# Linear attention and a top-2 mixture of experts: key transposes by single heads, gate products by quarters turned on VectorE

## The chip, the core and the metric

The kernel runs on one core of a Trainium2 chip. The metric is the device time of one execution in microseconds (us). The time of the kernel before is the median of three runs; the profile shows one execution of it.

## What is computed

First, decayed linear attention over 4 batches, 8 heads, 768 positions and 64 dimensions, in blocks with a carried state; then a mixture of 8 experts over the 3072 tokens of 512 features, of which each token uses two.

```python
intra = np.einsum('bhic,bhjc->bhij', qb, kb) * Dmask[None]
intra = np.einsum('bhij,bhjd->bhid', intra, vb)
inter = np.einsum('bhid,bhde->bhie', qb * lam_pow[None], kv_state)
out[:, :, sl] = intra + inter
kv_state = lam_block[None, :, None, None] * kv_state + np.einsum('bhsd,bhse->bhde', kb_dec, vb)

x = np.ascontiguousarray(attn_out.transpose(0, 2, 1, 3)).reshape(B * S, H * D)
logits = x @ w_gate
noise_scale = np.log1p(np.exp(x @ w_noise))
noisy_logits = logits + noise_scale * noise
# top 2 of 8 per token, softmax over the two as weights
h = np.maximum(x[mask] @ w1[e], 0.0)
out[mask] += top2_w[mask, k, None] * (h @ w2[e])
```

## The kernel before

**Stages.** The attention runs in 12 steps of 256 tokens (two chunks of 128; NST = 12), three steps to a batch. The loop over t (L981 to L1043) finishes step t and prepares step u = t + 1. Behind it the experts follow, one after the other, each as two matrix products over gathered token rows (gemm1, gemm2).

**One turn of the loop, in program order, which is the order on every engine.** The schedule is manual: instructions stand on each engine's queue as the code issues them.

1. trans_k(u) (L319): the keys of step u lie with two neighbouring positions and 64 dimensions of a head in one row. TensorE transposes 128 columns at a time into banks pS. Three sets of four transposes are made: one that takes the second position of one head and the first of the next, and two of which only one half is used. ScalarE (VectorE for u = 0) evacuates the three banks into kT, one in full, two by halves. In kT the index y mixes head parity and position, so scores (L372) reads kT at x ^ s.
2. kv(u) (L412): products of decayed keys and values; the first chunk goes to a bank pS, the second to bank pR. A step that ends a batch (u = 2, 5, 8, 11) has the first chunk alone. state(u) on VectorE (L431) adds them to the carried states.
3. trans_q(u) (L334): eight transposes; ScalarE copies them, VectorE scales them (qTs).
4. advance(FILLS): VectorE works off a budget of queued jobs (the gate of eight chunks, its routing, the lists of tokens), if there are any. Jobs are queued at t = 4, at t = 8 and after the loop, one group of tokens each (GB = 0, 8, 16, 24).
5. intra(t), inter(t, 0): the outputs of step t in banks pO and pKV; evac_o on ScalarE writes xo.
6. store_x(t - 1): eight transposes of xo, evacuated by ScalarE (xc) and stored by SyncE's DMA queue (SP) to x_tok in memory.
7. products(t - 1) (L434): gate and noise weights (32 columns) times xo. Four matmuls with 256 moving columns, one for each block of 128 features, each to its own 32 partitions of bank pR. ScalarE copies pR to xp (L440).
8. scores(u) (L372) into four banks pS; VectorE multiplies each by the decay mask (at, L375). Then inter(u, 1).
9. logits(t - 1) (L456): for each chunk one matmul with xp as weights and a selector of 16 columns (sel) adds the four blocks and turns tokens to partitions, into bank pL. The gate's first job copies the logits from there (L476).
10. advance(FILL): again a budget of jobs on VectorE.

There are four banks pS in rotation and one each of pR, pO, pKV and pL. A product into a bank waits until its last reader is done.

**Tokens and partitions.** In the gate, partition p of chunk c is token 128 c + p; noise (nz, L1043), the token numbers for the lists (rowf, tokb, L243 to L248, loads, decode) and the store of the gate weights (store_w, L548) all use this. store_w writes 8 weights of 4 bytes to each row of x_tok with one DMA per group; the expert gathers rows of x_tok afterwards.

**After the loop.** The first matmuls of expert 0 (mm1), products(11), store_w(1), store_x(11), the remaining jobs, logits(11), the lists (enlist, bank pR), and then the evacuations evac1 on ScalarE (L901) and VectorE (L905) into ht, which lies where xc lay before.

Of the kernel before, what the change touches and what calls it, by code (L numbers as in the profile page):

```python
# [21 lines left out]
FT = mybir.dt.float32  # L22
# [37 lines left out]
HOT = 2 * (128 + NTL + NV * NTL)  # L60
NST = NCH // 2
NW = NC // 2
MAXOV = 40
ARENA = 1304
MAXT = 24
OPUS = 0.21
FILL, SPLIT, FILLS = 2.0, 1.2, 3.4
# [25 lines left out]
def sub(ap, offset, dims):  # L93
    return bass.AP(tensor=ap.tensor, offset=ap.offset + offset, ap=dims)
# [31 lines left out]
def kernel(  # L126
# [90 lines left out]
    def mask(s, h, c):  # L217
# [25 lines left out]
    nc.gpsimd.iota(rowf, pattern=[[0, 1]], base=-TS, channel_multiplier=1, allow_small_or_imprecise_dtypes=True)  # L243
    tokb = consts.tile([128, NCH, NV], BF, name="tokb")
    nc.gpsimd.iota(tokb[:, :, 0], pattern=[[1, NCH]], base=-(BIG // TS), channel_multiplier=0,
                   allow_small_or_imprecise_dtypes=True)
    nc.gpsimd.iota(tokb[:, :, 1], pattern=[[0, NCH]], base=-TS, channel_multiplier=1,
                   allow_small_or_imprecise_dtypes=True)  # L248
    destf = consts.tile([128, 2, NCH], FT, name="destf")
    recs = consts.tile([128, NTL], I32, name="recs")  # L250
    sel = consts.tile([128, 2 * E], FT, name="sel")

    def make_sel():

        v = nc.vector
        v.tensor_scalar(sel, jp[:, 0:2 * E], 0.0, None, op0=OP.is_equal)
        for q in range(1, DB):
            v.tensor_scalar(sq4, jp[:, 0:2 * E], float(-32 * q), None, op0=OP.is_equal)
            v.tensor_add(sel, sel, sq4)

    sq4 = ac.tile([128, 2 * E], FT, name="sq4")

    class Arena:

        def __init__(self, n):
# [13 lines left out]
            return v  # L279

    arena = Arena(ARENA)
    for s, w in ((0, w_gate), (1, w_noise)):
# [33 lines left out]
    def half(i):  # L316
        return slice(i * 64, (i + 1) * 64)

    def trans_k(u, banks=()):  # L319

        banks = iter(banks)
        kT[u] = aw.tile([128, HP, 2, C], FT, name="kT", bufs=1)
        flat = KT[u].rearrange("p h x d -> p (h x d)")
        for at, y, r in ((D, 1, slice(0, 128)), (0, 0, half(0)), (2 * D, 0, half(1))):
            nm = next(banks, None)
            p = psum.tile([128, HP, C], FT, name=nm) if nm else bank()
            for hp in range(HP):
                nc.tensor.transpose(p[:, hp, :], flat[:, hp * 4 * D + at:hp * 4 * D + at + 2 * D], identf)  # L328
            if u:
                nc.scalar.activation(kT[u][r, :, y, :], p[r], AF.Copy)  # L330
            else:
                nc.vector.tensor_copy(kT[u][r, :, y, :], p[r])

    def trans_q(u, banks=()):  # L334

# [26 lines left out]
    def scores(u):  # L362
        AT[u] = []
        for r in range(2):
            at = aw.tile([128, 2, 2, 2, C], FT, name="at")
            AT[u].append(at)
            ps = [bank().rearrange("p (h x) i -> p h x i", x=2) for _ in range(2)]
            for h in range(2):
                for x in range(2):
                    for s in range(2):  # L370
                        for a in range(2):
                            nc.tensor.matmul(ps[s][half(a), h, x, :], kT[u][half(s), 2 * r + h, x ^ s, half(a)],  # L372
                                             qT[u][half(s), 2 * r + h, a * C:(a + 1) * C], start=True, stop=True)
            for s in range(2):
                nc.vector.tensor_mul(at[:, s], ps[s], mask(s, slice(2 * r, 2 * r + 2), slice(0, C)))  # L375
# [80 lines left out]
    def logits(u):  # L456
        nonlocal pl
        for a in range(2):
            g = 2 * u + a
            b = max(i for i in range(NG) if GB[i] <= g)  # L460
            if not g:
                pl = psum.tile([128, 512], FT, name="pL")
            if g == GB[b]:
                PL[b] = pl[:, NV * NTL:][:, :GM * 2 * E].rearrange("p (c e) -> p c e", e=2 * E)
                PC[b] = pl[:, NV * NTL + GM * 2 * E:]
            nc.tensor.matmul(PL[b][:, g - GB[b], :], XP[u][:, a, :], sel, start=True, stop=True)


    def gate(b):
# [4 lines left out]
        pl = PL[b]  # L474
        l2 = t([128, gs, 16], "l2")
        v.tensor_copy(l2, pl[:, :gs, :])  # L476
        yield
# [139 lines left out]
    def loads(b, c, n, buf):  # L617

        _, hi, mv = hot(buf, n)
        mv = mv.rearrange("p k (w j) -> p k w j", w=NV)  # L620
        nc.vector.tensor_scalar(mv[:, :, 1, :], hi, rowf, None, op0=MULT)
        for i in range(n):
            k = slice(2 * i, 2 * i + 2)
            nc.vector.tensor_scalar(mv[:, k, 0, :], hi[:, k, :], float(GB[b] + c + i - BIG // TS), None, op0=MULT)

    found = consts.tile([128, NV, NTL], FT, name="found")

# [15 lines left out]
    def decode(s, out, n):  # L643

        v = nc.vector
        idf = rp.tile([128, n], FT, name=f"idf{n > 1}")
        v.scalar_tensor_tensor(idf, s[:, 0], float(TS), s[:, 1], op0=MULT, op1=ADD)
        v.tensor_scalar(out, idf, float(BIG + TS), None, op0=ADD)

    def read_lists(a, b):  # L650
# [10 lines left out]
    kdecay(0)  # L661
    load(2, "kt")
    load(2, "vt")
    trans_k(1, ("pO", "pKV", "pL"))
    trans_q(1, ("pO", "pKV"))
    keep_warm(WARM[1])
    kv(0)
    kdecay(1)
# [13 lines left out]
        nc.vector.tensor_add(xo, xo, PO[0][0][half(g), g::2, :])  # L682
    kv(1)
    state(1)
    make_sel()
    inter(1, 1)

    def places(b):
# [292 lines left out]
    for t in range(NST):  # L981
# [16 lines left out]
        if not t:  # L998
            pass
        elif u < NST:  # L1000
            advance(FILLS)
        else:
            store_x(t - 1)
            products(t - 1)
            for j in range(PARTS0[0]):
                trans_rows(0, j)
            logits(t - 1)
            advance(FILLS)
        if t:
            intra(t)  # L1010
# [29 lines left out]
        if t >= NST - 2:  # L1040
            zero_out(3)
        if t == 2:
            nc.sync.dma_start(nz, sub(noise, 0, [[E, 128], [128 * E, NCH], [1, E]]))  # L1043
    assert got
    finish(1)
    head = [mm1(0, 0, PARTS0[0], 0)]
# [280 lines left out]
```

## Time and profile before

| | us |
|---|---|
| median of three runs | 718.95 |
| lowest and highest | 718.71, 720.71 |
| span of the profiled execution | 716.8 |
| TensorE busy | 698.8 |
| VectorE busy | 398.3 |
| GpSimd busy | 361.8 |
| ScalarE busy | 223.3 |

The span runs from the first to the last instruction of the profiled execution; no other time of its own is given for that execution, and the median lies 2.15 us above the span. The attention takes about the first 140 us, the experts the rest. The mean granted clock of TensorE is 0.994. Busy shares are averages over these stages, so a stage is read by itself.

### The profile page before, as it was taken

Reading aid. Unit: us, or ns where it says so; the run is one execution under the profiler, and the core shown is the slowest. Engines: PE = TensorE matmul, PEld = TensorE weight load, DVE = VectorE, ACT = ScalarE, POOL = GpSimd, SP = SyncE. Lnnn points to the kernel's source line nnn. Section 1 sums busy time; section 2 is a strip of 40 time slices with the busy share of each in tenths; the row PEclk is TensorE's granted clock in tenths of the full one; section 3 lists DMA queues with packets and bytes.
Section 4 is the critical chain, followed back from the end, with each engine's and each line's share of the span. In section 5 each row is a group of like instructions: output and inputs, shape, how many; then the busy total and the mean of one; then the engine's idle time right before and its main releaser. Section 6 shows DMA issues by size and latency. Waiting matters only on the chain.

```text
span 716.8 us, 15851 instructions
## 1 busy us (share of the span) xinstructions
PE 698.8 (97%) x6014; PEld 600.4 (84%) x6014; DVE 398.3 (56%) x1044; ACT 223.3 (31%) x382; POOL 361.8 (50%) x505
## 2 busy tenths in 40 slices
PE   7899999999999999999999999999999999999994
PEld 5888888889898898988888888888888898888883
DVE  4755899879355546743674367337624662565210
ACT  2255545542143312332233214222322242223100
POOL 4411342313453865687768567836773768321221
PEclk9999999999999999999999999999999999999998
DMA  9998986580645725273627352735452554330110
GB/s 203 263 230 245 251 232 203 188 305 25 180 131 168 207 56 179 82 185 87 183 93 176 85 186 84 176 88 161 116 154 79 170 143 122 104 116 30 51 51 32
DMA packets 94192, 104.32 MB, mean 146 GB/s; under 512 B 41234, under 2 KB 66844, under 8 KB 94112
## 3 DMA queue, kind: packets, MB, share of 16 engines
q1 hardware_dynamic: 79456, 65.73, 34.0%
q0 software_dynamic: 13552, 37.00, 17.0%
q10 hardware_dynamic: 1104, 0.53, 0.5%
q8 instruction: 49, 0.80, 0.5%
q14 instruction: 31, 0.25, 0.1%
HBM read 78.28 MB, written 26.12 MB: 146 GB/s over the span
## 4 chain that ended last, share of the span: by engine, by line
PE 89%; issue 4%; DMA 2%; POOL 1%; DVE 1%; ACTq 0%; SPq 0%; ACT 0%; POOLq 0%
PE pS L895 37%; PE pKV L933 16%; PE pO L933 16%; PE pO L384 3%; PE pS L372 3%; PE pS L328 2%; PE pS L450 2%; PE pO L938 2%; PE pS L419 2%; PE pS L344 1%; PE pKV L384 1%; PE pKV L938 1%; DMA Mk<-powd 1%; PE pR L438 1%; PE pS L874 1%
## 5 line engine op out<-in xcount | busy, mean ns | idle before, releaser
L839 POOL DMA_INDIRECT xg<-x_tok,recq x147 | 161.0, 1095 | 45.6 <-issue 40.0
L895 PE MATMUL pS<-xth,w1h 128*128 128x512 f32 (+3 forms) x544 | 181.4, 333 | 0.9 <-DVE ht L905 0.9
L895 PE MATMUL pS<-xth,w1l 128*128 128x512 f32 (+3 forms) x544 | 180.5, 332 | 0.0
L895 PE MATMUL pS<-xtl,w1h 128*128 128x512 f32 (+3 forms) x544 | 180.5, 332 | 0.0
L905 DVE SCALAR_TENSOR_TENSOR ht<-pS,ht 128x256 fp32r<-128x256 f32 (+3 forms) x176 | 75.8, 454 | 123.1 <-ACT ht L901 120.7
L933 PE MATMUL pKV<-w2h,ht 128*128 128x512 f32 x384 | 122.6, 390 | 0.0
L933 PE MATMUL pO<-w2h,ht 128*128 128x512 f32 x384 | 122.4, 390 | 0.0
L952 POOL DMA_INDIRECT out_dram<-ot,rec x46 | 60.7, 1319 | 121.0 <-DVE ot L945 110.8
L901 ACT ACTIVATE ht<-pS 128x512 fp32r<-128x512 f32 (+3 forms) x136 | 65.2, 483 | 173.2 <-PE pS L895 167.7
L895 PEld LDWEIGHTS pS<-xth,w1h 128*128 128x128 f32 x544 | 102.7, 189 | 10.4 <-DVE ht L905 1.1
L895 PEld LDWEIGHTS pS<-xth,w1l 128*128 128x128 f32 x544 | 102.7, 189 | 8.8
L895 PEld LDWEIGHTS pS<-xtl,w1h 128*128 128x128 f32 x544 | 102.7, 189 | 8.8
L933 PEld LDWEIGHTS pO<-w2h,ht 128*128 128x128 f32 x384 | 72.1, 188 | 14.9
L933 PEld LDWEIGHTS pKV<-w2h,ht 128*128 128x128 f32 x384 | 72.1, 188 | 14.9
L866 ACT ACTIVATE xth<-turned 128x512 fp32r<-128x512 f32 (+1 forms) x39 | 23.7, 607 | 167.5 <-DVE turned L864 167.5
L933 PE MATMUL pKV<-w2l,ht 128*128 128x512 f32 x192 | 74.9, 390 | 0.0
L933 PE MATMUL pO<-w2l,ht 128*128 128x512 f32 x192 | 74.8, 390 | 0.0
L360 POOL TENSOR_TENSOR kd<-kt,Mk 128x512 f32<-128x512 f32 x24 | 24.8, 1051 | 73.4 <-PE pR L419 51.6
L917 POOL DMA_INDIRECT pv<-out_dram,rec x46 | 47.0, 1021 | 14.2 <-issue 12.0
L375 DVE TENSOR_TENSOR at<-pS,Mk 128x512 f32<-128x512 f32 x48 | 29.9, 683 | 23.0 <-PE pS L372 18.5
L808 DVE TENSOR_TENSOR w2l<-wst,w2h 128x1024 fp32r<-128x1024 f32 (+1 forms) x33 | 39.2, 1191 | 6.1 <-ACT w2h L807 5.6
L933 PEld LDWEIGHTS pKV<-w2l,ht 128*128 128x128 f32 x192 | 36.1, 188 | 7.4
(241 smaller groups left out, 941.5 us busy)
## 6 DMA issues: line engine op xcount, KB each, us to landing
wst<-in_moe_w_dram SPq DMA_DIRECT2D x36, 512.0 KB, 4.2
wst<-in_moe_w_dram SPq DMA_DIRECT2D x96, 128.0 KB, 3.7
x_tok<-xc SPq DMA_DIRECT2D x24, 272.0 KB, 4.7
kt<-in_k_dram SPq DMA_DIRECT2D x12, 512.0 KB, 5.2
qt<-in_q_dram SPq DMA_DIRECT2D x24, 256.0 KB, 5.2
vt<-in_v_dram SPq DMA_DIRECT2D x12, 512.0 KB, 5.7
out_dram<-zero SPq DMA_DIRECT2D x24, 256.0 KB, 3.6
xg<-x_tok,recq POOLq DMA_INDIRECT x147, 2.8
```

The lines of the kernel that those rows point to most:

```text
L360: nc.gpsimd.tensor_mul(kd[:, :, s], kt[:, :, s], mask(s, slice(0, HP), slice(C - 1, C)).to_broadcast([128, HP, 2, D]))
L375: nc.vector.tensor_mul(at[:, s], ps[s], mask(s, slice(2 * r, 2 * r + 2), slice(0, C)))
L384: nc.tensor.matmul(PO[u][a][half(g), hp, :], lhs, rhs, start=n == 1, stop=n == (8 if not (u % NW or a) else 12 if u else 10))
L808: nc.vector.tensor_tensor(lo[:, r], st[:, r], hi[:, r].bitcast(FT), op=SUB)
L839: nc.gpsimd.indirect_dma_start(out=XG[t][:, g * QW:(g + 1) * QW], out_offset=None, in_=x_tok.rearrange("t (q w) -> (t q) w", w=QW), in_off ...
L866: nc.scalar.activation(hi, raw, AF.Copy)
L895: nc.tensor.matmul(p, W1[a][d][:, fs], xt(b, cs)[:, d], start=(d == 0 and i == 0), stop=(d == DB - 1 and i == 2))
L901: nc.scalar.activation(ht(e, 0, f, cs), p, AF.Relu)
L905: nc.vector.scalar_tensor_tensor(ht(e, 1, f, c), p[:, r], 0.0, ht(e, 0, f, c).bitcast(FT), op0=OP.max, op1=SUB)
L917: nc.gpsimd.indirect_dma_start(out=PV[t][:size(e, t), :], out_offset=None, in_=out, in_offset=bass.IndirectOffsetOnAxis(ap=REC[e, t], axis=0),
L933: nc.tensor.matmul(p, ht(e, a, f, cs), W2[b][f // 2][:, f % 2, :], start=(i == 0), stop=(i == len(terms) - 1))
L952: st = nc.gpsimd.indirect_dma_start(out=out, out_offset=bass.IndirectOffsetOnAxis(ap=REC[e, t], axis=0), in_=o, in_offset=None, bounds_che ...
```

## The change

Two things change together. **Keys:** one transpose takes one head with both positions, so eight transposes in two banks hold all keys. Each bank is evacuated as two halves of 64 partitions, which puts position x at index x of kT; scores reads it there. **Gate:** products(u) makes 16 matmuls of 64 moving columns: each quarter of the step's 256 tokens gets its own 32 partitions, and the four blocks of features are summed in place. There is no copy xp, no selector and no logits matmul; in their place VectorE turns bank pR in blocks of 32 x 32 straight into the gate's buffer (the arena, or lg1 for the second group). Partition p now means another token: 32 neighbouring partitions hold 32 neighbouring tokens, and neighbouring 32-blocks lie 64 tokens apart. So the noise load and each store of the gate weights become eight DMAs, the token numbers change, and GpSimd makes rowf and tokb by quarters. In the last step of the loop logits stands ahead of the row transposes, and one warm-up matmul (it writes pR) is added.

```diff
-        for at, y, r in ((D, 1, slice(0, 128)), (0, 0, half(0)), (2 * D, 0, half(1))):
+        for s in range(2):
             nm = next(banks, None)
             p = psum.tile([128, HP, C], FT, name=nm) if nm else bank()
             for hp in range(HP):
-                nc.tensor.transpose(p[:, hp, :], flat[:, hp * 4 * D + at:hp * 4 * D + at + 2 * D], identf)
-            if u:
-                nc.scalar.activation(kT[u][r, :, y, :], p[r], AF.Copy)
-            else:
-                nc.vector.tensor_copy(kT[u][r, :, y, :], p[r])
+                nc.tensor.transpose(p[:, hp, :], flat[:, (2 * hp + s) * 2 * D:(2 * hp + s + 1) * 2 * D], identf)
+            for x in range(2):
+                if u:
+                    nc.scalar.activation(kT[u][half(s), :, x, :], p[half(x)], AF.Copy)
+                else:
+                    nc.vector.tensor_copy(kT[u][half(s), :, x, :], p[half(x)])
...
-                            nc.tensor.matmul(ps[s][half(a), h, x, :], kT[u][half(s), 2 * r + h, x ^ s, half(a)],
+                            nc.tensor.matmul(ps[s][half(a), h, x, :], kT[u][half(s), 2 * r + h, x, half(a)],
...
-        p = psum.tile([128, 2, C], FT, name="pR")
+        p = XP[u] = psum.tile([128, 2, 32], FT, name="pR")
         for d in range(DB):
-            nc.tensor.matmul(p[d * 32:(d + 1) * 32], wgn[:, d, :], XO[u][:, :, d, :], start=True, stop=True)
-        XP[u] = aw.tile([128, 2, C], FT, name="xp", bufs=1)
-        nc.scalar.activation(XP[u], p, AF.Copy)
+            for j in range(4):
+                nc.tensor.matmul(p[j * 32:(j + 1) * 32], wgn[:, d, :], XO[u][:, j // 2, d, half(j % 2)],
+                                 start=d == 0, stop=d == DB - 1)
...
-            nc.tensor.matmul(PL[b][:, g - GB[b], :], XP[u][:, a, :], sel, start=True, stop=True)
+            if not a:
+                nc.vector.transpose(PL[b][:, g - GB[b]:][:, :2, :].rearrange("p g e -> p (g e)"),
+                                    XP[u].rearrange("p g r -> p (g r)"))
...
-        rows = x_tok[GB[b] * C:GB[b + 1] * C, :].rearrange("(c p) w -> p c w", p=128)
-        nc.sync.dma_start(rows[:, :, WAT:], RT[b].pop("w"))
+        w = RT[b].pop("w")
+        for j in range(4):
+            for g in range(2):
+                rows = x_tok[GB[b] * C + 64 * j + 32 * g:, :]
+                nc.sync.dma_start(sub(rows, WAT, [[XW, 32], [2 * C * XW, w.shape[1] // 2], [1, E]]),
+                                  w[j * 32:(j + 1) * 32, g::2, :])
...
             products(t - 1)
+            logits(t - 1)
             for j in range(PARTS0[0]):
                 trans_rows(0, j)
-            logits(t - 1)
+            keep_warm(1)
```

How the instructions move shows at three places. **TensorE, the step in which u = 4 is prepared:** from the transposes of xo over the gate products, the scores and inter to the keys and the KV products. Before:

```order
L450 MATMUL pS<-identf,xo 128x128 x8
L438 MATMUL pR<-xo,wgn 32x256 x4
L372 MATMUL pS<-qT,kT 64x128 x32
L384 MATMUL pKV<-qTs,S_148 64x128 x4
L466 MATMUL pL<-sel,xp 128x16 x2
L328 MATMUL pS<-identf,kt 128x128 x12
L419 MATMUL pS<-vt,kd 64x64 x2
L419 MATMUL pR<-vt,kd 64x64 x2
```

and now:

```order
L442 MATMUL pS<-identf,xo 128x128 x8
L431 MATMUL pR<-xo,wgn 32x64 x16
L364 MATMUL pS<-qT,kT 64x128 x32
L376 MATMUL pKV<-qTs,S_148 64x128 x4
L319 MATMUL pS<-identf,kt 128x128 x8
L411 MATMUL pS<-vt,kd 64x64 x2
L411 MATMUL pR<-vt,kd 64x64 x2
```

The logits pair is gone, four key transposes are gone, and between the gate products and the KV products, which both write pR, less stands than before.

**VectorE, the step in which u = 11 is prepared:** the mask products of u = 10, then the split of expert weights (w2l), jobs (MAX, MAX_INDEX), the states and qTs of u = 11. Before:

```order
L505 MAX arena<-arena 128x8
L375 TENSOR_TENSOR at<-pS,Mk 128x512 x4
L808 TENSOR_TENSOR w2l_515<-wst,w2h_511 128x1024
L505 MAX arena<-arena 128x8 x7
L508 MAX_INDEX arena<-arena 128x8
L431 SCALAR_TENSOR_TENSOR S_152<-S_151,QS,pS 128x64 x4
L351 TENSOR_TENSOR qTs<-pS,QS 128x4x128 x2
```

and now:

```order
L496 MAX arena<-arena 128x8 x3
L367 TENSOR_TENSOR at<-pS,Mk 128x512 x4
L459 STREAM_TRANSPOSE arena<-pR 128x64
L803 TENSOR_TENSOR w2l_505<-wst,w2h_501 128x1024
L496 MAX arena<-arena 128x8 x5
L499 MAX_INDEX arena<-arena 128x8 x3
L423 SCALAR_TENSOR_TENSOR S_152<-S_151,QS,pS 128x64 x4
L343 TENSOR_TENSOR qTs<-pS,QS 128x4x128 x2
```

The turn that empties pR stands behind the four mask products, and jobs have moved ahead by two or three small operations.

**SP's DMA queue, after the loop:** the stores of gate weights (from the arena) and of x. Before:

```order
L965 DMA out_dram<-zero 128x512 x3
L550 DMA x_tok<-arena 128x8x8
L454 DMA x_tok<-xc_183 128x544
L454 DMA x_tok<-xc_184 128x544
L965 DMA out_dram<-zero 128x512 x17
```

and now:

```order
L960 DMA out_dram<-zero 128x512 x3
L544 DMA x_tok<-arena 32x4x8 x8
L446 DMA x_tok<-xc_188 128x544
L446 DMA x_tok<-xc_189 128x544
L960 DMA out_dram<-zero 128x512 x17
```

The last two stores of x stand behind eight issues instead of one.

## Rows read from the trace of the kernel before

**Rows 1.** The page's head: span; busy us, share, instructions of each engine.

```profile
span 716.8 us, 15851 instructions
PE 698.8 (97%) x6014; PEld 600.4 (84%) x6014; DVE 398.3 (56%) x1044; ACT 223.3 (31%) x382; POOL 361.8 (50%) x505
```

**Rows 2.** Busy us (instructions) of each engine by stretch; clock, DMA share, GB/s.

```profile
60.00:70.00 10.00, 10.00 (x231) 8.68 (x231) 5.48 (x12) 5.09 (x10) 2.06 (x2) 1.00 0.85 243
70.00:130.00 60.00, 59.96 (x1429) 52.25 (x1430) 53.87 (x207) 31.80 (x59) 21.70 (x49) 1.00 0.75 215
130.00:150.00 20.00, 19.08 (x306) 16.77 (x304) 15.01 (x49) 11.68 (x25) 4.26 (x14) 1.00 0.81 280
```

**Rows 3.** Chain of waits in the loop: start us, us, engine, tile, line.

```profile
51.26 0.20 PE pS L419 x2
52.35 1.02 PE pS L344 x8
...
56.74 0.57 PE pR L438 x8
57.31 1.91 PE pS L372 x64
...
59.66 0.55 PE pL L466 x4
60.20 1.36 PE pS L328 x12
61.56 1.08 PE pS L419 x32
...
77.90 1.91 PE pS L372 x64
...
120.26 1.91 PE pS L372 x64
...
123.19 1.85 PE pS L328 x12
```

**Rows 4.** VectorE's timeline, mask products: start us, us, ..., [idle before <-releaser].

```profile
58.38 2.48 DVE L375 TENSOR_TENSOR at<-pS,Mk 128x512 f32<-128x512 f32 x4 [3.17 <-PE pS L372]
...
79.55 2.46 DVE L375 TENSOR_TENSOR at<-pS,Mk 128x512 f32<-128x512 f32 x4
...
100.00 2.48 DVE L375 TENSOR_TENSOR at<-pS,Mk 128x512 f32<-128x512 f32 x4 [0.24 <-PE pS L372]
...
122.46 2.46 DVE L375 TENSOR_TENSOR at<-pS,Mk 128x512 f32<-128x512 f32 x4
```

**Rows 5.** Groups by shape, VectorE's later transposes: count | busy us, mean ns.

```profile
L864 DVE STREAM_TRANSPOSE turned<-xg 128x512 f32<-128x512 f32 x36 | 25.3, 702 | 0.0
L864 DVE STREAM_TRANSPOSE turned<-xg 128x128 f32<-128x128 f32 x3 | 0.9, 302 | 0.0
```

**Rows 6.** Groups by shape, weight loads of the key transposes, 28-150 us.

```profile
L328 PEld LDWEIGHTS pS<-identf,kt 128*128 128x128 f32 x120 | 13.3, 145 | 0.7 <-DVE at L375 0.4 <-issue 0.2
```

**Rows 7.** Groups by shape, ScalarE's copies, 28-150 us.

```profile
L330 ACT ACTIVATE kT<-pS 64x512 f32<-64x512 f32 x20 | 11.7, 586 | 0.2
...
L440 ACT ACTIVATE xp<-pR 128x256 f32<-128x256 f32 x12 | 4.8, 404 | 1.6 <-PE pR L438 1.2 <-ACT xc L452 0.3
```

**Rows 8.** Timeline of SP's queue after the loop; the page's key loads.

```profile
141.97 0.38 SPq L550 DMA_DIRECT2D x_tok<-arena  x1
143.09 1.05 SPq L454 DMA_DIRECT2D x_tok<-xc  x2
...
kt<-in_k_dram SPq DMA_DIRECT2D x12, 512.0 KB, 5.2
```

**Rows 9.** Timeline of three engines at the first expert's evacuation.

```profile
146.31 0.66 ACT L901 ACTIVATE ht<-pS 128x256 fp32r<-128x256 f32 x2 [2.76 <-DMA x_tok<-xc]
...
148.51 0.76 DVE L905 SCALAR_TENSOR_TENSOR ht<-pS,ht 128x256 fp32r<-128x256 f32 x2
...
148.99 0.39 PE L895 MATMUL pS<-xth,w1h 128*128 128x256 f32 x1 [0.92 <-DVE ht L905]
```

More of the change, by code (lines that the diff above doesn't have):

```diff
@@ L62 @@
 NW = NC // 2
+QT32 = 32
 MAXOV = 40
-ARENA = 1304
+ARENA = 1432
 MAXT = 24
@@ L242 @@
     rowf = consts.tile([128, 1], FT, name="rowf")
-    nc.gpsimd.iota(rowf, pattern=[[0, 1]], base=-TS, channel_multiplier=1, allow_small_or_imprecise_dtypes=True)
     tokb = consts.tile([128, NCH, NV], BF, name="tokb")
[L245 to L248, printed above, removed]
+    nc.gpsimd.iota(tokb[:, :, 0].rearrange("p (u g) -> p u g", g=2), pattern=[[8, NST], [1, 2]], base=-(BIG // QT32),
+                   channel_multiplier=0, allow_small_or_imprecise_dtypes=True)
+    for j in range(4):
+        for o, n in ((rowf, 1), (tokb[:, :, 1], NCH)):
+            nc.gpsimd.iota(o[j * 32:(j + 1) * 32], pattern=[[0, n]], base=64 * j - TS, channel_multiplier=1,
+                           allow_small_or_imprecise_dtypes=True)
     destf = consts.tile([128, 2, NCH], FT, name="destf")
     recs = consts.tile([128, NTL], I32, name="recs")
[L251 to L261, printed above, removed]
     class Arena:
@@ L281 @@
     arena = Arena(ARENA)
+    lg1 = ac.tile([128, GM, 32], FT, name="lg1")
     for s, w in ((0, w_gate), (1, w_noise)):
@@ L463, in logits @@
             if g == GB[b]:
-                PL[b] = pl[:, NV * NTL:][:, :GM * 2 * E].rearrange("p (c e) -> p c e", e=2 * E)
-                PC[b] = pl[:, NV * NTL + GM * 2 * E:]
-            nc.tensor.matmul(PL[b][:, g - GB[b], :], XP[u][:, a, :], sel, start=True, stop=True)
+                PL[b] = lg1 if b == 1 else arena.tile([128, GM, 32], FT, name="l2")
+                PC[b] = pl[:, NV * NTL:]
+            if not a:
+                nc.vector.transpose(PL[b][:, g - GB[b]:][:, :2, :].rearrange("p g e -> p (g e)"),
+                                    XP[u].rearrange("p g r -> p (g r)"))
     def gate(b):
@@ L473, in gate @@
         t = lambda sh, nm, dt=FT: arena.tile(sh, dt, name=nm)
[L474 to L477, printed above, removed]
+        l2 = PL[b][:, :gs, :]
         zc = t(sh, "zc")
@@ L548, in store_w @@
     def store_w(b):
-        rows = x_tok[GB[b] * C:GB[b + 1] * C, :].rearrange("(c p) w -> p c w", p=128)
-        nc.sync.dma_start(rows[:, :, WAT:], RT[b].pop("w"))
+        w = RT[b].pop("w")
+        for j in range(4):
+            for g in range(2):
+                rows = x_tok[GB[b] * C + 64 * j + 32 * g:, :]
+                nc.sync.dma_start(sub(rows, WAT, [[XW, 32], [2 * C * XW, w.shape[1] // 2], [1, E]]),
+                                  w[j * 32:(j + 1) * 32, g::2, :])
     def count(b):
@@ L623, in loads @@
             k = slice(2 * i, 2 * i + 2)
-            nc.vector.tensor_scalar(mv[:, k, 0, :], hi[:, k, :], float(GB[b] + c + i - BIG // TS), None, op0=MULT)
+            nc.vector.tensor_scalar(mv[:, k, 0, :], hi[:, k, :], float((GB[b] + c + i) // 2 * 8 + (c + i) % 2 - BIG // QT32), None,
+                                    op0=MULT)
     found = consts.tile([128, NV, NTL], FT, name="found")
@@ L646, in decode @@
         idf = rp.tile([128, n], FT, name=f"idf{n > 1}")
-        v.scalar_tensor_tensor(idf, s[:, 0], float(TS), s[:, 1], op0=MULT, op1=ADD)
+        v.scalar_tensor_tensor(idf, s[:, 0], float(QT32), s[:, 1], op0=MULT, op1=ADD)
         v.tensor_scalar(out, idf, float(BIG + TS), None, op0=ADD)
@@ L663 @@
     load(2, "vt")
-    trans_k(1, ("pO", "pKV", "pL"))
-    trans_q(1, ("pO", "pKV"))
+    trans_k(1, ("pO", "pL"))
+    trans_q(1, ("pKV", "pO"))
     keep_warm(WARM[1])
@@ L684 @@
     state(1)
-    make_sel()
     inter(1, 1)
@@ L1042 @@
         if t == 2:
-            nc.sync.dma_start(nz, sub(noise, 0, [[E, 128], [128 * E, NCH], [1, E]]))
+            for j in range(4):
+                for g in range(2):
+                    nc.sync.dma_start(nz[j * 32:(j + 1) * 32, g::2, :],
+                                      sub(noise, (64 * j + 32 * g) * E, [[E, 32], [2 * C * E, NST], [1, E]]))
     assert got
```

## The prediction

> **What bounds the kernel now.** I read the page's head first: TensorE is busy 698.8 of a span of 716.8 us [rows 1]. Then the stretches: in the attention loop TensorE has no idle time, 59.96 of 60 us between 70 and 130 us, and VectorE already works 53.87 of those 60 [rows 2]; before 70 us VectorE is half idle (5.48 of 10). So time taken off TensorE is gained only as far as VectorE, next in line, can follow. Third the chain of waits, which in the loop is a list of TensorE's pieces and prices each [rows 3]; fourth VectorE's timeline, which shows where it waits for the scores (58.38: 3.17 us; 100.00: 0.24) and where it comes to them late (79.55 and 122.46: no wait) [rows 4]. After the loop the expert products keep TensorE busy to the end, and the change leaves them alone: what is gained must be gained before 150 us.
>
> I call u the step whose keys are being turned, and count each point's gain: how much earlier it comes than before. Only profiled rows go into the sum, so it is made against the span of 716.8 us and the difference is set against the median of 718.95 (2.15 us lie around the span).
>
> **TensorE's part.** Twelve key transposes take 1.36 us; eight take 0.91, so 0.45 goes in each of ten loop steps. The two logits products take 0.55 a step and go too, in as many steps [rows 3]. The gate's products stay at 1,024 columns but become 16 matmuls with 64 columns, 32 passes instead of 8. The KV products have such passes of 64 columns: 64 of them (32 matmuls of two passes) between 51.26 and 52.35, 0.017 each with four parts of the array in use, and 32 in 1.08, 0.034 each, with two [rows 3]. So the products cost between 32 x 0.017 = 0.54 and 32 x 0.034 = 1.08, against 0.57 now: -0.03 to +0.51. I take 0.65, +0.08, near the first: four strips of the array are used in turn, as now. A step thus loses 0.45 + 0.55 - 0.08 = 0.92 us on TensorE.
>
> All passes of the products use the same 128 rows of the array. The key transposes do too, and their weight loads last 0.145 us each [rows 6], yet one passes every 0.113 us [rows 3]: load and product overlap. The Trainium skill ("TensorE: Matmul & The Clock Gate", section on packing small matmuls) says that a load overlaps a running matmul only where the row groups differ; by its P/1.2 ns, 32 columns make an estimated 27 ns a load, 0.85 us a step in the open, and little of the 0.92 would be left. The trace of this kernel disagrees, with those 0.113 us against 0.145.
>
> **VectorE's new place on the path.** ScalarE used to empty bank pR right after the products. Now the turn on VectorE empties it, and stands behind the four mask products of the scores (the order of VectorE above). Its price: 128x512 takes 702 ns and 128x128 takes 302 [rows 5], about 1.05 ns a column, so 0.23 for 64 columns; the ends are 0.15 (half of the 302) and 0.30. The next KV products write pR, except in u = 5, 8, 11, which have one chunk. In a light step: scores start, VectorE begins 1.07 later (57.31, 58.38), its four products take 2.4 until the next can start (2.48 less the overlap of neighbours), the turn 0.23, the signal 0.1 (estimate): pR is free 3.8 us after the scores' start. TensorE now gets there after 1.91 + 0.44 (57.31 to 59.66) + 0.91 = 3.26. It waits 0.55 where it waited for nothing. So a step with pR gains 0.92 - 0.55 = 0.37, one without gains 0.92.
>
> **Where VectorE itself is late.** In u = 6 the scores start at 77.90 and VectorE at 79.55, where 78.97 would be on time: it is 0.58 late already, and TensorE has a second bank of scores to fill meanwhile [rows 3, 4]. There TensorE comes 0.37 sooner, and VectorE has the turn more (its logits copy goes, one small operation moves ahead of the scores; about 0.1 in all): it will be 1.0 late, and banks and pR with it. In u = 10 it is 1.1 late now (120.26, 122.46), and the keys of u = 11 start late for it: their twelve show 1.85 us instead of 1.36 [rows 3]. TensorE coming 0.92 sooner makes it 2.1. In u = 8 the wait of 0.24 turns into 0.2 to 0.3 of lateness [rows 4].
>
> Step by step the gain at the KV products is: u = 3: 1.1 (one wait of 0.3, the first step is longer); 4: 1.4; 5: 2.3; 6: 2.7; 7: 2.1 (VectorE 1.0 late); 8: 3.0; 9: 3.3; 10: 4.2 (the list's products cover the wait); 11: 3.8.
>
> **After the loop.** In the last step two logits pairs more go (0.9), products and the new warm-up matmul add 0.4, and that matmul writes pR and so waits about 1.1 (estimate) for a turn that stands behind a weight split and four routing operations on VectorE: gain 3.2. Then the expert's first evacuation. It now waits 2.76 us for x_tok's transfers, but VectorE's part, at 148.51, is what TensorE stops for (0.92) [rows 9]. On SP's queue the weights' store becomes eight issues: two take 1.05 [rows 8], so eight about 3.6 instead of 0.38; x_tok behind them is issued and lands some 2.4 later against the queue's own start. ScalarE has 1.7 us in hand there (done at 146.7, wanted at 148.4), so about 0.4 comes through (0 to 1.5). Gain at the end: **2.9 us**.
>
> **Costed at nothing.** The noise load and the first weights' store also become eight issues, 3.2 us on SP; the keys, queries and values behind them are wanted a step of 10 us later and land in 5.2 [rows 8]. ScalarE gets a fourth half evacuation (586 ns) and loses the copy of 404 ns [rows 7]; it works 31.8 of 60 us [rows 2]. GpSimd's six more iotas stand before its wait for the masks; the selector's seven VectorE operations go before a wait for KV products. Without these covers they would cost under 1 us each.
>
> **Rivals.**
> - *The saving goes through.* VectorE has 6.1 us idle in 70 to 130 [rows 2]; if its waits shrink instead of TensorE's growing, all comes through: 10 x (0.45 + 0.55) - 12 x 0.08 = 9.0, time 709.9. Against it: the idle time lies in other steps than the late ones, and the pR wait is there with an idle VectorE too. Chance 0.10.
> - *Nothing measurable.* With the turn at 0.30, products at +0.2, and the two late steps passing to the next, every pR step gains 0.2 or less and the rest goes into u = 7 and 11: gain 1.0, time 718.0. For it: VectorE at 90% in six steps. Chance 0.30.
> - *Slower: weight loads in the open.* If the 32 small loads of a step stand between the products, these take more than now. A load of 128 columns lasts 0.145 us [rows 6], so one of 32 columns 0.036, and 24 more of them 0.87: 1.5 us a step, +0.93. It decides from +0.45: then a pR step gains nothing. At +0.93 pR steps lose 0.48 each and u = 5, 8, 11 gain 0.07; with the end it comes to about 2.4 lost, time 721.4. For it: 16 loads instead of 4 on the same rows; against it the overlap of the key transposes. Chance 0.10. The Trainium skill's rule on row groups would give about this time.
>
> **The numbers.** The forecast (TensorE paced by VectorE, 0.50) gives 718.95 - 2.9 = 716.0, its own range 713.8 to 717.5 with the bounds of turn, products and stores. A measurement here tells 0.3%, 2.2 us, from no change. The whole range 712.0 to 720.0 leaves out the saving that goes through and the slower case. Faster 0.58 (nearly all of the forecast and the first rival), within 0.3% 0.32, slower 0.10.
>
> **What would show it.** In the profile after: key transposes 0.91 a step, no logits products, gate products at 0.6 to 0.7; TensorE waiting about 0.5 us at the KV products' bank pR for VectorE's turn in u = 3, 4, 6, 9; the mask products of u = 6 and u = 10 starting without a wait, and TensorE waiting over 1 us for them; VectorE above 92% between 70 and 125 us; evacuations of the first expert delayed behind x_tok. It is wrong if TensorE waits for nothing in the loop (the first rival), or if products take over 1 us (the slower one).

## The result: slower by 1.2%, and the profile after

The changed kernel takes **728.1 us** (median of 4 runs, 726.9 to 728.8), the kernel before 718.9 beside it: ratio **1.0119, 95% interval 1.0104 to 1.0133**. The forecast was 716.0, the range 712 to 720. The profiled execution has a span of 726.9, 10.1 us more than before.

The head of the page after [rows 1]:

```profile
span 726.9 us, 16272 instructions
...
PE 697.3 (96%) x6207; PEld 599.2 (82%) x6207; DVE 403.6 (56%) x1047; ACT 227.3 (31%) x381; POOL 362.1 (50%) x511
```

TensorE works 1.5 us less than before, in a span that is 10.1 us longer: the time went into idling. The stretches of [rows 2], after:

```profile
60.00:70.00 10.00, 8.91 (x223) 7.64 (x219) 5.76 (x12) 5.52 (x10) 2.06 (x2) 1.00 0.90 232
70.00:130.00 60.00, 53.84 (x1452) 46.74 (x1444) 53.66 (x182) 30.67 (x53) 19.53 (x37) 1.00 0.80 226
130.00:150.00 20.00, 19.38 (x442) 16.92 (x441) 16.80 (x68) 9.95 (x18) 6.74 (x25) 0.91 0.47 165
```

Between 70 and 130 TensorE, idle for 0.04 us before, now idles 6.2. VectorE is no busier (53.66 against 53.87). Between 130 and 150 the granted clock is 0.91, where it was 1.00. What TensorE waited for between the scores of u = 2 (38.38) and of u = 11 (138.31); columns are line, releaser, us, times, longest. The same question to the trace of before, for its 36.16 to 131.06, has no line in answer.

```profile
PE pS L319 <- DVE at L367: 3.0, 2, 2.3
PE pR L431 <- issue: 1.0, 1, 1.0
PE pKV L376 <- issue: 0.9, 1, 0.9
PE pL L553 <- issue: 0.8, 1, 0.8
PE pR L411 <- DVE lg L459: 0.4, 1, 0.4
PE pR L411 <- DVE arena L496: 0.4, 1, 0.4
PE pR L411 <- issue: 0.3, 1, 0.3
```

"issue" is a stop for which the trace shows no event that TensorE waited for. The chain of waits after, against [rows 3], from the prologue on:

```profile
25.96 1.91 issue
...
30.37 1.90 PE pS L319 x8
...
58.22 0.58 PE pR L431 x32
58.80 1.91 PE pS L364 x64
61.15 1.02 PE pS L319 x8
...
68.01 0.47 PE pR L431 x24
68.48 0.98 issue
69.46 0.32 PE pR L431 x8
...
89.56 0.94 issue
...
95.10 0.80 issue
...
129.47 1.25 PE pS L319 x8
130.72 1.34 PE pS L411 x32
132.07 1.90 PE pS L336 x8
...
157.67 7.50 PE pS L890 x48
```

In an undisturbed step products take 0.58, keys 1.02 to the KV products (1.44 before, for twelve), and the logits are gone. At 129.47 the keys of u = 11 come 2.3 us after TensorE was ready; what follows runs at a lower clock (eight q transposes take 1.90 instead of 1.02). The 48 matmuls behind the first evacuation take 7.50 where they took 6.01.

The 10.1 us by place, from when the same event comes in both traces:

| from | to | before | after | lost |
|---|---|---|---|---|
| start | scores of u = 2 | 36.16 | 38.38 | 2.2 |
| there | scores of u = 11 | 94.90 | 99.93 | 5.0 |
| there | restart of the first expert [rows 9] | 17.93 | 19.36 | 1.4 |
| there | its 48 matmuls done | 6.01 | 7.50 | 1.5 |

Behind that nothing more is lost.

The first row is a stop and the clock behind it. The KV products of u = 1 stop at 25.96 for 1.91 us. VectorE, free at 27.84 (27.35 before), waits 0.88 us for them, and behind the gap TensorE's granted clock is 0.75 between 30 and 35 (1.00 before): the eight keys of u = 2 take 1.90. turn_first and same_tokens (below), which turn these keys in the same way, stop at the same place for 1.31 and 2.21 us but keep a clock of 1.00 between 30 and 35; their scores of u = 2 start at 36.38 and 37.20.

In the second row nine steps save 7.9 us of TensorE's segments (keys 3.7, logits 4.2), and 12.9 come in again: between scores and keys 4.2 (the waits for the mask products, 3.0, and a stop), between the start of the KV products and q 4.5 (pR, and stops), between q and the transposes of xo 2.5 (a stop, and the clock in u = 11), in the products 1.5 (a stop of 0.98 and shorter ones), elsewhere 0.2. These parts are worked out from the starts of each step's groups in TensorE's two timelines.

### The profile page after: what moved, and what is told of

It is laid out like the page before. It is cut to its first block, busy times and chain, and to the rows that moved or that the text cites. A ratio compares the mean times of both kernels' runs of the same rounds, so it can differ in the third digit from the quotient of the medians.

```text
span 726.9 us, 16272 instructions
## 1 busy us (share of the span) xinstructions
PE 697.3 (96%) x6207; PEld 599.2 (82%) x6207; DVE 403.6 (56%) x1047; ACT 227.3 (31%) x381; POOL 362.1 (50%) x511
## 4 chain that ended last, share of the span: by engine, by line
PE 81%; DVE 7%; issue 5%; POOL 1%; DMA 1%; SPq 1%; ACT 0%; POOLq 0%; DVEq 0%; ACTq 0%
PE pS L890 37%; PE pKV L928 16%; PE pO L928 16%; DVE at L367 2%; PE pO L376 2%; PE pO L933 2%; PE pS L364 1%; PE pS L336 1%; PE pKV L933 1%; PE pS L411 1%; PE pS L442 1%; POOL out_dram L947 1%; DVE arena L102 1%; PE pS L869 1%; PE pS L319 1%
## 5 line engine op out<-in xcount | busy, mean ns | idle before, releaser
L912 POOL DMA_INDIRECT pv<-out_dram,rec x46 | 47.1, 1024 | 14.3 <-issue 8.7
L928 PEld LDWEIGHTS pO<-w2l,ht 128*128 128x128 f32 x192 | 36.1, 188 | 7.3
```

The source lines that it names most:

```text
L912: nc.gpsimd.indirect_dma_start(out=PV[t][:size(e, t), :], out_offset=None, in_=out, in_offset=bass.IndirectOffsetOnAxis(ap=REC[e, t], axis=0),
L928: nc.tensor.matmul(p, ht(e, a, f, cs), W2[b][f // 2][:, f % 2, :], start=(i == 0), stop=(i == len(terms) - 1))
```

## Experiments

Three readings of the traces had to be told apart: GpSimd holds VectorE up; TensorE stops for want of instructions; the prologue is late. Ratios are against the kernel before in the same session, in brackets the 95% interval. That kernel took 719 us in three of the six sessions and 731 to 739 in the other three (one chip gave 719 in one session and 739 in another), where idle time among the experts and a lower clock behind it were added; so spans are compared within the loop, "the loop" being the time from the scores of u = 2 to those of u = 11 in the one profiled execution of each kernel.

### The two parts alone

keys_only is the kernel before with the change's `trans_k` and `scores`; gate_only is the change with those of before.

> The kernel before with the keys' part alone (eight transposes in two banks, evacuated by halves; the prologue's banks as in the change). Theory A (the turn on VectorE keeps bank pR and puts the loop on VectorE's pace, which the gate's part alone brings): this kernel loses nothing in the loop, TensorE's 0.45 us a step come through where VectorE is not late, span 713 to 716, no idle of TensorE at bank pR. Theory B (the loss comes with the keys: prologue +1.6 us, and half evacuations that make kT late): span 718 to 721. Theory C (the engines wait for instructions, which follows the number of TensorE's instructions a microsecond): the keys' part has fewer instructions, so no idle of kind 'issue' on TensorE.

> The change with the keys' part undone (twelve transposes in three sets as before). Theory A: span 720 to 725, most of the 10.1 us of the change are here. Theory B: span 716 to 718. Theory C: as much 'issue' idle on TensorE as in the change (about 4.7 us), since the 16 products a step are here.

keys_only: **1.0073** (1.0051 to 1.0095), span 723.2, loop 98.73, against 94.90 before. gate_only: **1.0106** (1.0078 to 1.0135), span 721.9, loop 98.84. So either part alone loses: theories A and B, which put the loss into one of them, both fall. Both show stops of kind "issue" in the loop (keys_only 1.8 us, gate_only 4.6; the change 3.0) and one more in the prologue (2.0 and 0.9), though keys_only has fewer instructions: their number alone is not it.

### GpSimd's kd against VectorE

VectorE's timeline in the kernel before, start of u = 10's jobs:

```profile
114.86 0.48 DVE L101 SCALAR_TENSOR_TENSOR arena<-arena 128x64 f32<-128x64 f32 x2
115.26 0.15 DVE L647 SCALAR_TENSOR_TENSOR idfTrue<-found 128x2 f32<-128x2 f32 x1
```

and GpSimd's there:

```profile
115.49 2.06 POOL L360 TENSOR_TENSOR kd<-kt,Mk 128x512 f32<-128x512 f32 x2 [8.84 <-PE pR L419]
```

The same place in keys_only, VectorE:

```profile
116.96 1.32 DVE L101 SCALAR_TENSOR_TENSOR arena<-arena 128x64 f32<-128x64 f32 x2
118.21 1.02 DVE L648 SCALAR_TENSOR_TENSOR idfTrue<-found 128x2 f32<-128x2 f32 x1
```

and GpSimd:

```profile
117.15 2.06 POOL L361 TENSOR_TENSOR kd<-kt,Mk 128x512 f32<-128x512 f32 x2 [9.63 <-PE pR L420]
```

The first pair ends at 118.28, the second operation at 119.23; the two kd end at 118.18 and 119.21. An operation on two words a partition takes 1.02 us instead of 0.15, until a kd is done. In the kernel before kd starts, as always, when the KV products release its buffer, and VectorE is then at the states and qTs, whose inputs are partly in PSUM and which it does not touch. With TensorE earlier relative to VectorE, kd meets the jobs, which read and write SBUF. The Trainium skill ("SBUF — State Buffer", section on who interferes with whom) says that a VectorE instruction with two SBUF inputs contends with a GpSimd instruction that reads SBUF, and that the second to issue is blocked until the first is done. The trace agrees: 0.87 us of wait for 0.15 of work. In the change six such places (74.96, 86.65, 87.75, 108.72, 109.59, 119.51) cost VectorE 5.5 us above the usual lengths, casts and tensor_scalar operations among them (86.65, 108.72); in the kernel before one costs 0.75.

kd_after makes kd wait for VectorE's first state:

```diff
             state(u)
+            nc.gpsimd.tensor_copy(spacer, SA[u, 1][0:1, 0, 0:1])
             kdecay(t + 2)
```

> The change, and in the loop GpSimd copies one word of step u's first new state before it starts the decayed keys (kd), so that kd runs beside VectorE's state and qTs operations, which read PSUM. Theory E (kd starts as soon as the KV products are done; TensorE being earlier, it now meets VectorE's jobs that read and write SBUF, each of which then waits for the end of a kd of 1.03 us; that costs VectorE 5.1 us between 70 and 125 us against 0.8 before, and the lateness in u = 10 and the clock lost behind it): VectorE's operations are back at their usual lengths, the excess is under 1 us, scores of u = 11 start 2.5 to 5 us earlier than in the change (138.3), span 722 to 724.5. Rival (VectorE is late by the sum of its work, the turn included): the excess moves into waits, span 726 to 728.

Measured: **1.0030** (0.9999 to 1.0061). VectorE's operations are back at their lengths (at the last place):

```profile
118.70 0.74 DVE L102 SCALAR_TENSOR_TENSOR arena<-arena 128x64 f32<-128x64 f32 x3
```

(2.25 in the change), the sum above the usual lengths is 0.8 us, TensorE's wait at the keys of u = 11 is 0.4 us instead of 2.3, the granted clock stays at 1.00 between 120 and 150, and the loop takes 96.21, 3.7 less than in the change; the scores of u = 11 start 3.9 us earlier, at 134.46. That is with 4.6 us of stops in the loop, where the change has 3.0. Theory E holds for the loop. The span of 732.7 that was expected at 722 to 724.5 is that session's: from the restart of the first expert on it takes 578.7 us, the change 569.2, with 3.5 us of stops among its experts. In the same session q_late (below), which has the change's loop without the wait, took 1.0112. Worked out in the same way, VectorE's sum is 3.9 to 5.6 us in the five other kernels with a part of the change and no wait for kd (3.9 in gate_only, 5.6 in keys_only: either part moves kd), and 0.6 to 1.3 in the seven others with it. Over all kernels with the whole change the loop took 99.9 to 102.8 without this wait (four kernels) and 94.7 to 99.2 with it (four); of the keys' part 98.7 without and 93.2 to 96.6 with it (four).

### Stops for instructions

before_split and before_strips are the kernel before with 16 gate products of 64 columns, as in the change, and nothing else.

```diff
-            nc.tensor.matmul(p[d * 32:(d + 1) * 32], wgn[:, d, :], XO[u][:, :, d, :], start=True, stop=True)
+            for j in range(4):
+                nc.tensor.matmul(p[d * 32:(d + 1) * 32, j // 2, half(j % 2)], wgn[:, d, :], XO[u][:, j // 2, d, half(j % 2)],
+                                 start=True, stop=True)
```

> The kernel before, only each gate product of 256 moving columns split into four of 64 (16 matmuls a step, as in the change); bank, ScalarE's copy, logits and everything else are as before. Theory C (TensorE stops at every 256th or so instruction when the next block of instructions has not arrived; more instructions in less time bring it on): TensorE's own time changes by under 0.1 us a step, but idle of kind 'issue' appears on TensorE, 1 to 4.6 us in all, span 718 to 722. Rival (the stops belong to the change's other parts): no idle of that kind, span within 0.7 us of 716.8 plus 12 times the products' difference.

Measured: **1.0075** (1.0041 to 1.0108). The products take 1.32 us a step, because four matmuls in a row go to the same 32 columns of the array; 0.75 more than before, and the test of the stops is spoilt: TensorE is slower. There is one of 0.8 in the prologue and none in the loop, with as many matmuls as before_strips. before_strips swaps the loops, `for j` outside `for d`, so that neighbours go to different columns:

> As before_split (the kernel before, gate products in 16 matmuls of 64 columns), but with the blocks of features in the inner loop, so that one matmul after the other goes to another 32 columns of the array. The products should then take 0.58 us a step as in the change, and not 1.35. Theory C (instructions arrive too late when more of them are used up in less time): idle of kind 'issue' on TensorE in the loop, 1 to 4 us in all, ratio 1.002 to 1.006. Rival: none in the loop, ratio 0.998 to 1.001.

Measured: **1.0018** (0.9984 to 1.0052; the total decides nothing), products 0.58, loop 100.12, 5.2 more than before. TensorE's waits in its loop:

```profile
PE pR L439 <- issue: 2.1, 2, 1.7
PE pS L419 <- issue: 1.3, 1, 1.3
PE pS L328 <- issue: 0.4, 1, 0.4
```

3.8 us of stops, in a kernel whose arithmetic is that of before. Where they stand tells what they are. Stretches of all_loop (below), each cut at a stop; the counts behind TensorE's two entries are its matmul passes and its weight loads:

```profile
44.40:64.40 20.00, 19.46 (x509) 17.15 (x506) 12.37 (x28) 12.86 (x23) 4.40 (x6) 1.00 1.06 244
64.40:70.00 5.60, 4.65 (x130) 3.92 (x127) 3.13 (x8) 2.03 (x5) 0.00 (x0) 1.00 0.78 244
70.00:74.80 4.80, 4.19 (x128) 3.74 (x127) 4.11 (x17) 2.21 (x4) 2.20 (x3) 1.00 0.83 238
74.80:81.00 6.20, 5.67 (x128) 4.75 (x126) 5.59 (x21) 2.62 (x5) 0.00 (x0) 1.00 0.93 265
...
85.50:105.70 20.20, 19.18 (x507) 16.74 (x505) 15.57 (x45) 12.75 (x22) 9.51 (x31) 1.00 0.80 218
...
111.60:116.40 4.80, 4.48 (x129) 3.93 (x127) 4.38 (x15) 1.58 (x3) 0.00 (x0) 1.00 0.82 258
```

From stop to stop are 128 passes and as many loads, or four times that: 256 instructions, or 1,024, within about 1% of the records. The stops of the change show the same (515 passes between 68.40 and 89.50, 128 to 95.05), in the middle of a row of matmuls that wait for nothing; and from its stop in the prologue to that of 68.48 there are 2,019 recorded, eight times 256 less 1.4%. The page counts the packets that bring instructions (packets, MB, share), before and after:

```profile
q8 instruction: 49, 0.80, 0.5%
q8 instruction: 50, 0.82, 0.5%
```

That is 16.3 to 16.4 KB a packet, and over all kernels 48 to 51 packets for 11,932 to 12,604 passes and loads of TensorE: about one for 256. The Trainium skill ("Runtime: NRT & Kernel Launch", section on instruction fetch) says that instructions are fetched by DMA in blocks of 16 KiB, 256 of them, and that this stays hidden because they are issued more slowly than they come. The blocks agree; "hidden" does not: up to 2.2 us of TensorE stand in the open at one block's end.

before_load asks whether data transfers make the blocks late; it is the kernel before and two more stores a step:

```diff
         load(t + 3, "vt")
+        if 0 < t < NST - 2:
+            for i in range(2):
+                nc.sync.dma_start(out[i * 128:(i + 1) * 128, :], zero[:, :DM])
```

> The kernel before, with two more stores of 256 KB of zeros a step on SP's queue (to rows that are written again later). Theory C with transfers as its cause (the blocks of instructions come by the same DMA engines and land late when these are full): idle of kind 'issue' on TensorE in the loop, 0.5 to 4 us, where the kernel before has none; also waits for q, k or v if their loads become late. Rival (only the density of instructions counts): no idle of that kind.

Measured: **1.0058** (1.0037 to 1.0078), loop 97.35, and stops, where TensorE's instructions are those of before:

```profile
PE pS L372 <- issue: 1.0, 2, 0.6
PE pS L344 <- issue: 0.5, 1, 0.5
```

So both seem to count: instructions that are used up faster, and DMA queues that are fuller. Each rests on one execution, and that a stop is a wait for a late block is inferred from its place; no row shows the block land. before_again, the control, has none in the loop:

> The kernel before, unchanged, as one more profile and as a measure of the comparison itself: ratio 1.000 within its interval. Theory C: no idle of kind 'issue' on TensorE if its absence belongs to the kernel; if it is an accident of one execution, 1 to 4 us of it.

Measured: 0.9987 (0.9946 to 1.0028), loop 95.02. Its experts show idle time of kind "issue" in that session, after 150 us:

```profile
PE pS L895 <- issue: 5.6, 12, 1.2
```

These gaps are of another sort. Those from 255 to 267 us lie 1 to 8 matmuls and loads apart, not 256, and the granted clock is 0.64 between 256 and 268; TensorE works 7.6 us more in this execution than in the first one of that kernel (706.4 against 698.8). Their cause stays open.

### Token order, turn, prologue

same_tokens lets quarter j take 32 tokens of each chunk, so that the tokens stay where they were and each noise load and weight store is one DMA:

```diff
-                nc.tensor.matmul(p[j * 32:(j + 1) * 32], wgn[:, d, :], XO[u][:, j // 2, d, half(j % 2)],
+                nc.tensor.matmul(p[j * 32:(j + 1) * 32], wgn[:, d, :], XO[u][:, :, d, j * 32:(j + 1) * 32],
```

> The change, but a quarter's 64 moving columns are 32 of each chunk, so that partition p of chunk c stays token 128 c + p: noise load and weight stores are one DMA each again, and token numbers as before. Theory A: the loop up to 140 us is as in the change, the end gains the 4.3 us by which SP's queue and x_tok are later only as far as VectorE allows: span 724 to 726. Theory D (the sixteen and eight small DMAs make the loss, on SP's queue and by slowing the supply of instructions): span 717 to 720 and no 'issue' idle.

Measured: **1.0125** (1.0088 to 1.0162), span 725.1: theory D falls, the stops stay. But TensorE's wait for ht is 0.9 as before, where the change has 2.6. The change's end, SP's queue, then VectorE and TensorE at the first evacuation, against [rows 8, 9]:

```profile
149.07 4.64 SPq L544 DMA_DIRECT2D x_tok<-arena  x8
153.81 0.85 SPq L446 DMA_DIRECT2D x_tok<-xc  x2
...
157.19 0.76 DVE L900 SCALAR_TENSOR_TENSOR ht<-pS,ht 128x256 fp32r<-128x256 f32 x2 [1.65 <-DMA out_dram<-zero]
...
157.67 0.39 PE L890 MATMUL pS<-xth,w1h 128*128 128x256 f32 x1 [2.56 <-DVE ht L900]
```

Eight issues take 4.64 us, x_tok starts behind them, and 1.6 us more reach TensorE.

turn_first puts `logits(t - 1)` ahead of `scores(u)`.

> The change with the turn of step t-1 issued right behind the products, ahead of the mask products. Theory A: pR is free before the scores end, no wait of TensorE at pR for the turn; but in the steps where VectorE is late (u = 6 and 10) nothing is gained, since VectorE's sum of work is the same: span 722 to 725. Theories C and D: no difference from the change, 726 to 728.

Measured: **1.0098** (1.0065 to 1.0131), span 727.8, loop 102.83. No wait for the turn is left at pR, and nothing is gained: TensorE meets the mask products instead (3.2 us at the keys). So it is VectorE's lateness that decides there (3.5 us in u = 10), and not the place of the turn; its operations beside kd are 5.0 us over their usual lengths here too.

q_late moves the load of q(2) behind that of k(2).

> The change, but in the prologue the loads of q(2) are issued behind those of k(2), which wait for the decay masks. Theory F (the eight transposes of k(0) let go of q's buffer earlier, so the load of q(2) gets ahead of the masks' loads on the DMA engines, which land 1.7 us later): ScalarE's four mask issues take about 2.6 us instead of 4.9, the mask products of u = 0 end near 19.2 instead of 20.9, keys of u = 2 start near 29 instead of 30.3; span 724.5 to 726. Rival (the prologue is late by VectorE's four half copies, 0.8 us): mask issues and span as in the change within 0.5 us.

Measured: **1.0112** (1.0075 to 1.0150); ScalarE's mask issues still take 4.5 us (v(1) stands in q(2)'s place) and the keys of u = 2 start at 30.77. Theory F is not borne out. What all six kernels with the new keys in the prologue and ScalarE's masks share is TensorE's wait of 2.3 us for qT (1.07 before): VectorE empties u = 0's keys in four halves, 2.80 us instead of 2.01. What they share too is the stop in the KV products of u = 1, 1.3 to 2.2 us (none to 1.7 in the eight kernels with the old keys). Their keys of u = 2 start at 29.3 to 30.8, those of the eight at 27.6 to 30.1. In the change the stop and the clock behind it make most of the 2.2 us; how the order of the transfers bears on the stop stays open.

### Mended versions

keys_best, all_best and before_best have kd_after, the masks on SP's queue and q(0) copied by ScalarE; all_best is the whole change with same_tokens.

> The kernel before with the keys' part alone, and three moves: GpSimd's kd waits for the first new state (as in kd_after), the decay masks are loaded by SP's queue ahead of q(2) instead of by ScalarE's, and ScalarE, then free, copies q(0). Theories E and F (the keys' saving of 0.45 us a step is real and was eaten by the collisions of kd with VectorE and by the masks being late): keys of u = 2 start at 28 to 29 instead of 30.5, the excess of VectorE's operations is under 1 us, TensorE does not wait 1.8 us at the keys of u = 11; against the kernel before 3 to 5 us less, ratio 0.993 to 0.996. Rival (what is saved on TensorE is always lost elsewhere in the loop): ratio 1.000 or above.

> The whole change with the three moves of keys_best and the token order of same_tokens. Theories E and F with C: VectorE and the prologue are mended (4 + 2 us) and the end too (1.7 us), but TensorE's stops for instructions stay (2 to 5 us): ratio 1.000 to 1.004. If C is wrong and the stops go with the rest: ratio 0.992 to 0.996.

> Control: the kernel before with the same three moves and nothing of the change. VectorE's excess there is 0.8 us and its masks were on time, so theories E and F expect little: ratio 0.996 to 1.000. If the three moves gain as much here as in keys_best, they are gains of their own and say nothing of the change.

Measured: keys_best 0.9986 (0.9939 to 1.0034), all_best 1.0013 (0.9969 to 1.0057), before_best 1.0041 (1.0003 to 1.0080). The loops: 93.44, 99.24 (with 6.2 us of stops) and 95.64. In the loop the three moves gain the kernel before nothing, so what they gain there belongs to the change. The new prologue gained nothing reliable: keys of u = 2 at 31.35, 31.26 and 27.49.

keys_loop and all_loop leave the prologue's keys as before:

```diff
-    trans_k(0)
+    trans_k3(0)
...
-    trans_k(1, ("pO", "pL"))
+    trans_k3(1, ("pO", "pKV", "pL"))
```

> The kernel before; steps 0 and 1 turn their keys in three sets as before (so the prologue is the one of before), the other ten in two sets as in the change, and kd waits for the first new state. The theory (the keys' saving is real, collisions and prologue ate it): keys of u = 2 start within 0.5 us of the kernel before, VectorE's excess is under 1 us, from the keys of u = 2 to the scores of u = 11 it takes 1.5 to 4.5 us less than before's 102.4, ratio 0.994 to 0.998. Rival (the loop takes back what TensorE gains, by waits or stops for instructions): that stretch within 1 us of 102.4, ratio 0.999 or above.

> The whole change with the prologue's keys as in the kernel before, kd behind the first new state, and the token order of same_tokens. If the supply of instructions is all that is left: TensorE's idle of kind 'issue' in the loop is 2.5 to 5.5 us, the stretch from the keys of u = 2 to the scores of u = 11 is longer than in keys_loop by about that less the gate's own saving (0.3 to 0.9 us a step), ratio 1.000 to 1.004. If the turn on VectorE is a cause of its own: waits of TensorE at pR or at the mask products of over 2 us in sum.

Measured: keys_loop **0.9989** (0.9972 to 1.0007), loop 96.58, 3.6 us of stops; all_loop **1.0009** (0.9990 to 1.0028), loop 97.23, of which TensorE works 90.34 and stops 6.3. With VectorE and prologue mended, the change saves TensorE 4.4 us in the loop (94.78 worked before), and the stops for instructions take more than that back.

keys_front, all_front: the same two with the masks and q(0) of keys_best.

> keys_loop with the decay masks on SP's queue ahead of q(2) and q(0) copied by ScalarE. The prologue should gain 1 to 2 us (keys of u = 2 at 27 to 28 instead of 28.7 to 29.0), the stops for instructions stay (2 to 4 us in the loop): ratio 0.996 to 0.9985. Rival (an earlier loop meets fuller DMA queues and stops longer): ratio 0.999 or above.

> all_loop with the same prologue. Keys of u = 2 near 27.5, stops of 5 to 7 us in the loop: ratio 0.998 to 1.001.

> keys_front once more. If the gain belongs to the kernel: ratio 0.993 to 0.9985 also where the kernel before takes 719 us. If it belongs to that chip (stops for instructions among the experts, which the kernel before has more of there): ratio 0.998 to 1.001.

Measured: 0.9931 (0.9896 to 0.9965) and 0.9933 (0.9898 to 0.9967) where the kernel before took 739 us, and keys_front again **0.9988** (0.9974 to 1.0003) where it took 719. The first expectation's gain is therefore that session's, whose cause was not looked into; on the others no version is shown to beat the kernel before.

## Why the prediction was wrong

- **TensorE's part: right.** Keys to KV products fell by 0.42 (forecast 0.45), the logits' stretch by 0.46 (0.55), products cost 0.58 (0.65). The loads of the 32 columns overlap although they use the same 128 rows: 32 of them, 109 ns each, lie within 0.49 us. That is against the rule on row groups in the Trainium skill ("TensorE: Matmul & The Clock Gate", section on packing small matmuls), as the prediction took it; the third rival is out.
- **The wait at pR: right.** VectorE's and TensorE's timelines in u = 3:

```profile
41.92 0.23 DVE L459 STREAM_TRANSPOSE arena<-pR 128x64 f32<-128x64 f32 x1
```

```profile
41.74 0.33 PE L411 MATMUL pS<-vt,kd 64*64 64x64 f32 x4
42.20 0.27 PE L411 MATMUL pR<-vt,kd 64*64 64x64 f32 x2
```

  The turn takes 0.23 as forecast and pR's products start 0.44 late (0.55 forecast; 0.46 in u = 4).
- **"Where VectorE itself is late": the step that failed.** It let VectorE's work keep its length while TensorE came earlier. In u = 6 the masks start 1.4 us later than on time (82.59 for scores at 80.13, 1.07 apart; forecast 1.0), in u = 10 3.4 (128.75 for 124.29; forecast 2.1). Not the turn did that but kd, moved by the earlier KV products onto VectorE's SBUF work. kd_after shows it: there the two are 0.98 and 1.96, nearly as forecast, and the loop takes 3.7 us less, of the 5.0 that were lost.
- **A term that was missing: instructions.** The sum had no place for TensorE stopping between two matmuls that wait for nothing: 1.9 us in one stop in the change's prologue, 2.7 in three stops of over 0.5 in its loop, 6.3 in all_loop's. The number of instructions was never set against the time in which they are used.
- **"Costed at nothing".** VectorE's fourth half copy in u = 0 was not named (2.80 us for 2.01). The prologue came out 2.2 us later, but at the state of u = 1 VectorE was only 0.5 late: the rest is the stop there and the clock behind it. Eight issues took 5.54 (noise) and 4.64 (weights) where 3.2 and 3.6 were forecast; the row used, 1.05 for two, gives 4.2.
- **After the loop.** 0.4 was to come through; 1.6 did (2.56 against 0.92), and behind that idle time the granted clock was 0.94 and 0.96 (150 to 160, 160 to 190; 1.00 before): the next 48 matmuls took 1.5 longer.
- **The range** ended at 720: its only slower rival was one that the trace already spoke against.

## What to carry to other kernels

When one engine is made faster in a full loop, list what its earlier finish releases on the others, and beside which instructions that will then run: an operation on GpSimd that touched nothing before can hold up VectorE's SBUF work for its whole length. Count instructions per microsecond too, block by block, where matmuls are short and DMA queues full. And an idle gap on TensorE can cost twice, when the matmuls behind it run at the lower clock.

## What the runs showed of the hardware

- 32 passes of 64 columns take 0.58 us when neighbours go to different 32 columns of the array, and 1.32 when four in a row share them.
- TensorE's stops in the attention come at multiples of 256 instructions, 0.3 to 2.2 us each, also in the kernel before where transfers are added (before_load: 255, 1,010, 253 and 1,773 recorded passes and loads from stop to stop). The idle time among the experts (before_again) does not.
- A VectorE operation of 0.15 us waited until a kd of 1.03 us was done; S and qTs, with an input in PSUM, did not (four S in 0.85 us beside a kd in the kernel before, at 115.53).
- Behind a wait of 2.3 us TensorE's clock fell: 0.83 granted between 130 and 140, eight transposes in 1.90 instead of 1.02 us, which is the level of 1.2 instead of 2.4 GHz. Behind the prologue's stops it fell in the change (1.91 us; 0.75 between 30 and 35) and stayed at 1.00 in same_tokens (2.21 us).
- On SP's queue a DMA of 4 or 12 KB holds the queue about as long as one of 272 KB: 0.43 and 0.47 us (medians) against 0.34. Single issues of each kind took 1.4 to 1.8, and so eight came to 4.64 and 5.54.
